# Rows of an attention output projection moved between the head loop and its tail, in a four-layer attention and Fourier kernel

## The chip, the cores and the metric

The kernel runs on one core of one Trainium2 chip. The metric is the device time of one execution in microseconds (us). A core has a matrix engine (TensorE, PE in the profile, with its weight loads shown apart as PEld), a vector engine (DVE), an activation engine (ACT), a GpSimd engine (POOL) and a sync engine (SP), from whose queue this kernel issues every transfer (DMA). The kernel writes out the order of the instructions on each engine by hand, and each engine works through its own list strictly in that order.

## The reference

Four layers over 2048 rows of 640 numbers: attention, Fourier mixing, attention, Fourier mixing, each on the normalised rows and added to them.

```python
def _A_ref(x, wqkv, wo):
    B, S, D = x.shape
    H = 32; Dh = D // H; W = 256
    ...
    scores = jnp.einsum("bhqd,bhkd->bhqk", q, k) * (Dh ** -0.5)
    ...
    mask = (idx[:, None] - idx[None, :] >= 0) & (idx[:, None] - idx[None, :] < W)
    scores = jnp.where(mask[None, None], scores, -1e9)
    p = _softmax(scores, axis=-1)
    o = jnp.einsum("bhqk,bhkd->bhqd", p, v)
    return (lambda x, *d: x.transpose(*d))(o, 0, 2, 1, 3).reshape(B, S, D) @ wo
...
x = x + _A_ref(_layernorm(x, axis=-1), A_wqkv, A_wo)
x = x + _B_ref(_layernorm(x, axis=-1), B_dft_seq_re, B_dft_seq_im, B_dft_hid_re, B_dft_hid_im)
x = x + _A_ref(_layernorm(x, axis=-1), A_wqkv, A_wo)
x = x + _B_ref(_layernorm(x, axis=-1), B_dft_seq_re, B_dft_seq_im, B_dft_hid_re, B_dft_hid_im)
```

## The kernel before

All products are made from numbers cut into a high and a low part, so a term `a @ b` takes three matmuls (high by high, high by low, low by high).

**The head loop** (`heads`). The 32 heads are taken in 8 groups of four (quads), and each quad in 16 blocks of 128 rows: 128 steps. In step t the loop makes, on PE, the transposed scores of block t (line 657), and the plain scores of the block 10 steps ahead (line 629), whose row maxima DVE takes (line 634). Every four steps the maxima of four blocks are transposed (line 642), copied by ACT to a small tile `mt`, and stored by a DMA (line 647) as an additional row of `qp`, the queries. The transposed scores need this row. ACT takes the exponentials (line 667), POOL zeroes what is outside of the window (lines 673 and 677), and PE multiplies by the values (line 692, 24 small matmuls, one group to a step) for the block one step back. In a trace the groups of line 692 count the steps.

**What fills PE in the steps.** Each step has one place, after the first half of its scores, where `fill(nf)` puts in other PE work: first the query and key projections of later heads (`project`, chunks 2 to 9 of 128 columns, matmuls on half the array, two at a time, line 255), then the output projection `@ wo`. The output projection has 16 row blocks and a contraction in five chunks (`CHUNKS`). Chunks 0 to 2 need heads 0 to 23 alone and are the "early" part (`partials`, `EARLY = 3`): one early row is a row block's 18 matmuls of 128x320 (36 on half the array), and DVE adds the result to the residual `y` (line 975), which a DMA has loaded (`load_y`, line 949). Chunks 3 and 4 need the last quads and are the "late" part (`late`, 12 matmuls to a row, lines 237 and 1069 or 1075); behind a late row follow the statistics and the normalisation for the Fourier layer. `fill(9)` (`LATE = 9`) puts in half an early row to a step. `BACK = 2` holds two early rows back until the loop has ended, and lets two late rows into it.

**Sets.** For four row blocks at a time `load_o` loads the heads' outputs (`x<-o_d` or `cr<-o_d`) and the reciprocals of their sums (`rr<-r_d`), multiplies them (POOL in the loop, DVE later, line 890) and cuts them. `prepare` loads and cuts the weights and the first set while the last projection chunk is made.

**Behind the loop** (`after_heads`). The early rows that are left, then late rows and the first units of the Fourier layer in turn (line 1380, 9 matmuls of 512 columns).

**Queues and order.** `post(n, f)` runs `f` n half steps later, `job` puts it in a lane that gives out one job for each engine and half step. All DMAs stand in one list on SP. Eight semaphores go round, so a DMA is not issued before the one eight places ahead of it in the list has landed. `pack` (line 592) loads the queries and keys of a quad from where the projection was stored (`qk_d<-c`, line 522), in four groups of three DMAs for each quarter of the rows; the list `due` says at which step each quarter is loaded and how much of the projection must be done by then.

## Time and profile before

| what | us |
|---|---|
| median of 3 runs (2198.74 to 2204.55) | 2202.13 |
| the profiled execution's own time | 2201.15 |
| its span, on which all the rows lie | 2199.4 |
| first attention layer: from the last projection work to the end of the head loop | 412 to 534 |
| first attention layer: late rows and first Fourier units | 534 to 600 |
| the same two stretches in the second attention layer | 1502 to 1624, 1624 to 1690 |
| PE busy in 412 to 440, of 28 us | 23.73 |
| PE busy in 650 to 700, of 50 us | 50.00 |

A row of a stretch gives, engine by engine, the busy time in it and the number of instructions; then the clock that TensorE was granted (1.00 is full), the share of the DMA engines' time and the GB/s. A row of the timeline gives the start, the time and the engine of an instruction or of several alike; in square brackets stands how long the engine had been idle before it, and what ended that.

### The profile page before, as it was taken

Reading aid. Unit: us, or ns where it says so; the run is one execution under the profiler, and the core shown is the slowest. Engines: PE = TensorE matmul, PEld = TensorE weight load, DVE = VectorE, ACT = ScalarE, POOL = GpSimd, SP = SyncE. Lnnn points to the kernel's source line nnn. Section 1 sums busy time; section 2 is a strip of 40 time slices with the busy share of each in tenths; the row PEclk is TensorE's granted clock in tenths of the full one; section 3 lists DMA queues with packets and bytes.
Section 4 is the critical chain, followed back from the end, with each engine's and each line's share of the span. In section 5 each row is a group of like instructions: output and inputs, shape, how many; then the busy total and the mean of one; then the engine's idle time right before and its main releaser. Section 6 shows DMA issues by size and latency. Waiting matters only on the chain.

```text
span 2199.4 us, 48840 instructions
## 1 busy us (share of the span) xinstructions
PE 2127.3 (97%) x17872; PEld 1785.7 (81%) x17872; DVE 1620.9 (74%) x3949; ACT 1139.1 (52%) x2125; POOL 969.0 (44%) x1568
## 2 busy tenths in 40 slices
PE   7999999998999999999999999999999999999999
PEld 7987777677868888889999777776777788888899
DVE  6358888786897868776661688887868968687776
ACT  3117776656554545552431377676655545455332
POOL 3037776765513223232330477677655133231324
PEclk9999999999999999999999999999999999999999
DMA  5556656785435453665646466668753354546643
GB/s 182 175 162 186 201 181 207 224 221 164 161 122 171 138 185 127 221 199 194 208 146 188 149 199 183 201 195 231 216 170 135 128 187 135 166 152 207 226 161 127
DMA packets 220175, 392.09 MB, mean 178 GB/s; under 512 B 39200, under 2 KB 85792, under 8 KB 219936
## 3 DMA queue, kind: packets, MB, share of 16 engines
q1 hardware_dynamic: 219936, 388.98, 56.4%
q8 instruction: 141, 2.31, 0.4%
q14 instruction: 98, 0.80, 0.1%
HBM read 273.94 MB, written 113.77 MB: 176 GB/s over the span
## 4 chain that ended last, share of the span: by engine, by line
PE 79%; DVE 7%; ACT 4%; DMA 4%; POOL 3%; issue 3%; SPq 0%; ACTq 0%; DVEq 0%; POOLq 0%
PE banks L1380 29%; PE banks L237 15%; PE banks L255 13%; PE banks L692 6%; PE banks L657 5%; PE banks L1668 5%; PE banks L629 4%; DVE banks L634 1%; DMA qp<-qk_d 1%; DVE qp L230 1%; ACT pt L667 1%; DMA qk_d<-c 1%; PE banks L339 1%; POOL rs L1084 1%; ACT big L1036 1%
## 5 line engine op out<-in xcount | busy, mean ns | idle before, releaser
L634 DVE CUSTOM_DVE_ANT_0 banks<-banks,mask 128x384 f32<-128x384 f32 (+2 forms) x1024 | 527.4, 557 | 120.2 <-PE banks L629 97.3
L667 ACT ACTIVATE pt<-banks 128x768 f32<-128x768 f32 (+2 forms) x512 | 393.7, 772 | 172.0 <-PE banks L657 66.4
L673 POOL TENSOR_SCALAR_AFFINE_SELECT pt<-pt 128x256 f32<-128x256 f32 x512 | 214.7, 420 | 217.5 <-ACT pt L667 197.8
L255 PE MATMUL banks<-big,wc 64*128 64x512 f32 x1920 | 270.8, 394 | 0.4 <-DVE pt L440 0.4
L657 PE MATMUL banks<-qp,kp 61*128 61x384 f32 (+2 forms) x1024 | 210.8, 382 | 24.8 <-DVE mc L634 17.6
L692 PE MATMUL banks<-pt,vq 128*32 128x128 f32 x5760 | 212.0, 278 | 3.5 <-ACT pt L667 3.5
L629 PE MATMUL banks<-kp,qp 60*128 60x384 f32 (+2 forms) x1024 | 205.6, 346 | 4.7 <-DVE mc L634 3.0
L255 PEld LDWEIGHTS banks<-big,wc 64*128 64x128 f32 x1920 | 185.7, 185 | 23.5 <-ACT x L542 1.5
L224 ACT ACTIVATE qp<-pt 128x512 fp32r<-128x512 f32 (+1 forms) x201 | 124.0, 625 | 140.2 <-DVE pt L1314 56.7
L677 POOL TENSOR_SCALAR_AFFINE_SELECT pt<-pt 128x256 f32<-128x256 f32 x448 | 194.0, 433 | 0.0
L692 PEld LDWEIGHTS banks<-pt,vq 128*32 128x32 f32 x5760 | 142.5, 110 | 51.4 <-issue 35.6
L230 DVE TENSOR_TENSOR qp<-pt,qp 128x512 fp32r<-128x512 f32 (+1 forms) x199 | 153.8, 781 | 41.0 <-ACT qp L224 39.3
L657 PEld LDWEIGHTS banks<-qp,kp 61*128 61x128 f32 x1024 | 108.6, 185 | 90.0 <-DVE mc L634 63.9
L1313 POOL TENSOR_TENSOR pt<-pt,pt 128x512 f32<-128x512 f32 x34 | 50.6, 1488 | 241.3 <-DMA pt<-c 166.4
L1380 PE MATMUL banks<-qp,big 128*128 128x512 f32 x648 | 154.5, 392 | 0.0
L224 ACT ACTIVATE c<-pt 128x512 fp32r<-128x512 f32 x144 | 89.3, 625 | 120.3 <-POOL pt L1300 56.4
L629 PEld LDWEIGHTS banks<-kp,qp 60*128 60x128 f32 x1024 | 123.8, 186 | 30.5 <-DVE mc L634 18.2
L634 DVE DVE_READ_ACCUMULATOR2_ANT mc<- 128x1 f32 x1024 | 145.0, 142 | 0.0
L1380 PEld LDWEIGHTS banks<-qp,big 128*128 128x128 f32 x648 | 121.5, 189 | 25.2 <-POOL qp L230 0.9
L230 DVE TENSOR_TENSOR c<-pt,c 128x512 fp32r<-128x512 f32 x142 | 113.9, 804 | 26.9 <-ACT c L224 24.3
L1380 PE MATMUL banks<-qp,xc 128*128 128x512 f32 x480 | 119.0, 394 | 6.5 <-DVE xc L230 3.7
L1380 PEld LDWEIGHTS banks<-qp,xc 128*128 128x128 f32 x480 | 90.2, 189 | 28.5 <-DVE xc L230 6.3
(248 smaller groups left out, 4464.5 us busy)
## 6 DMA issues: line engine op xcount, KB each, us to landing
pt<-c SPq DMA_DIRECT2D x188, 512.0 KB
qk_d<-c SPq DMA_DIRECT2D x80, 512.0 KB
kp<-qk_d SPq DMA_DIRECT2D x384, 80.0 KB
qp<-qk_d SPq DMA_DIRECT2D x384, 80.0 KB
kp<-u_d SPq DMA_DIRECT2D x32, 640.0 KB
o_d<-ou SPq DMA_DIRECT2D x64, 256.0 KB
x_d<-x SPq DMA_DIRECT2D x48, 320.0 KB
v_d<-pt SPq DMA_DIRECT2D x16, 768.0 KB
```

The lines of the kernel that those rows point to most:

```text
L224: nc.scalar.activation(hi, src, AF.Copy, scale=-1.0 if neg else 1.0)
L230: (eng or nc.vector).tensor_tensor(out=lo, in0=src, in1=hi.bitcast(F32), op=OP.subtract)
L237: self.nc.tensor.matmul(p, x, y, start=n == 0, stop=n == last)
L255: self.nc.tensor.matmul(ps[a], x[r], y[r], start=half + i == 0, stop=half == 1 and i == n - 1, skip_group_check=True)
L629: nc.tensor.matmul(p, qp[quad % 2][b:b + 60, z, qb * P:(qb + 1) * P], kp[quad % 2][b:b + 60, z, k0 * P:(qb + 1) * P], start=True, stop=True)
L634: nc.vector.tensor_tensor_reduce(out=p, in0=p, in1=self.mask[:, 384 - n * P:], scale=1.0, scalar=NEG, op0=OP.add, op1=OP.max, accum_out=mc ...
L657: nc.tensor.matmul(self.banks[:, banks[e], :n * P], kp[quad % 2][b:b + 61, z, kb * P:(kb + 1) * P], qp[quad % 2][b:b + 61, z, kb * P:(kb + ...
L667: nc.scalar.activation(pt[quad, kb][:, 2 * z:2 * z + 2, :n * P], self.banks[:, b0:b1 + 1, :n * P], AF.Exp, scale=SCALE)
L673: nc.gpsimd.affine_select(out=t[:, :, 0:P], in_=t[:, :, 0:P], pattern=[[0, 2], [1, P]], compare_op=OP.is_ge, fill=0.0, base=0, channel_mul ...
L677: nc.gpsimd.affine_select(out=t[:, :, 256:384], in_=t[:, :, 256:384], pattern=[[0, 2], [-1, P]], compare_op=OP.is_gt, fill=0.0, base=0, ch ...
L692: nc.tensor.matmul(self.banks[32 * h:32 * h + 32, bank, :P], vq[:, 96 * (kb % 4) + 21 * h:96 * (kb % 4) + 21 * h + 32], t[:, h, (qb - kb) ...
L1380: nc.tensor.matmul(self.banks[:, bk, :], p, b[q], start=start and m == 0, stop=stop and last and m == 2, skip_group_check=True)
```

## The change

The pieces of the diff in which the order of work is decided:

```diff
-LATE = 9
-BACK = 2
+LATE = (9, 5), (9, 9)
+BACK = 4
+FEW = 2
+LAST = [(c, sbs) for sbs in ((0, 1), (2, 3)) for c in (NCH - 2, NCH - 1)]
...
         for lane in self.lanes.values():
-            for _ in range(2 if self.lead else 1):
+            for _ in range(2 if self.lead or self.wide else 1):
...
     def project(self):
-        for c in range(2, NCH):
+        for c in range(2, NCH - 2):
...
-                if c == NCH - 1:
-                    self.prepare(sbs[0])
                 yield from self.pieces(c, sbs, "f" if lead else "m")
-        self.prepare(4)
+        for c, sbs in LAST:
+            if (c, sbs) == LAST[0]:
+                self.load_chunk(NCH - 1)
+                self.post(6, lambda: self.cut_chunk(NCH - 1))
+            if (c, sbs) == LAST[2]:
+                self.prepare()
+            yield from self.pieces(c, sbs, "m")
+        self.take_big(2, F32)
+        self.load_y(range(AHEAD_X))
...
-            if not self.left:
-                if self.part_t < NB - BACK:
-                    self.now = self.out if self.ready_part() else None
+            if not self.left and not self.open:
+                if self.late_t < 2 and self.ready_late():
+                    self.now = self.rest
                 else:
-                    self.now = self.rest if self.late_t < BACK and self.ready_late() else None
+                    self.now = self.out if self.part_t < NB - BACK and self.ready_part() else None
...
-                    size = -(-left // max(1, round(left / n)))
+                    size = -(-left // max(1, round(left / n[self.side])))
...
-                nf = LATE
+                nf = LATE[s >= steps]
...
         for i in range(n):
-            self.post(7, lambda i=i: self.job(lane, key, lambda: scale(i)))
+            self.post(7 if busy else 4, lambda i=i: self.job(lane, key, lambda: scale(i)))
...
+    def early_ks(self, sb):
+        return range(FEW if sb == 0 else EARLY)
+
+    def prepare(self):
+
+        self.take_big(0)
+        self.take_big(1)
...
+        def load(k):
+            raw = self.raw()
+            self.nc.sync.dma_start(raw, self.a["wo"][:, k, :])
+            self.post(6, lambda: self.cut_job("dve", "ew", *self.early_w[k], raw))
+
+        def first(k):
+            o["left"] -= 1
+            self.load_o(o, 0, k)
+        for at, f, k in ((3, load, 0), (5, first, 0), (7, load, 1), (9, first, 1), (11, load, 2)):
+            self.post(at, lambda f=f, k=k: f(k))
...
+    def late_ks(self, sb):
+        return range(len(self.early_ks(sb)), KC)
...
-        while self.one_part():
-            pass
         self.load_to(4 if self.late_t < 8 else 6)
+        while self.part_t < NB - 1:
+            self.one_part()
...
             if t == NB:
                 break
+            self.one_part()
```

The first four early rows take two chunks instead of three; the third chunk of these rows goes to their late part. The last four pieces of the projection are made in another order (both chunks of the first half of the rows, then both of the second), two quarters of `pack` come two steps later, and weights and first set are loaded sooner. A later early row is spread over three steps (18, 10 and 8 half-array matmuls) until the plain scores have ended. Four early rows are left behind the loop instead of two, and three of them stand right behind it. Two late rows go into the loop in place of early ones as soon as their set is marked ready, and in the last ten steps sets are multiplied three half steps sooner and lanes give out two jobs.

**SP's list around the residual rows.** In the list of transfers, `big` are the residual rows `y`, `kp` and `qp` the loads of `pack`, `vq` the values, `x` and `rr` the heads' outputs and their factors, `c` the pieces of the projection on their way to memory, `sm`, `o_d` and `r_d` the results of a finished quarter, `mt` the row maxima. Before, from `vq` to the next `mt`:

```order
L619 DMA vq_91<-v_d 128x384
L949 DMA big_5879<-x 128x640 x4
L592 DMA qp_105<-qk_d 20x2x512 x3
L522 DMA qk_d<-c 128x2x512
L709 DMA sm<-ou_98 128x1x16
L710 DMA o_d<-ou_98 128x512
L715 DMA r_d<-rc 128x16
L592 DMA kp_103<-qk_d 20x2x512 x3
L522 DMA qk_d<-c 128x2x512
L647 DMA qp_105<-mt 2x4x128 x2
```

Now, from the same `vq`, and after `sm`, `o_d` and `r_d` on to the same `mt`:

```order
L631 DMA vq_91<-v_d 128x384
L967 DMA big_5871<-x 128x640 x5
L875 DMA x<-o_d 128x1x512
L883 DMA rr_100<-r_d 128x1x512
L875 DMA x<-o_d 128x1x512
L604 DMA kp_560<-qk_d 20x2x512 x3
L528 DMA qk_d<-c 128x2x512
```

```order
L604 DMA qp_105<-qk_d 20x2x512 x3
L604 DMA kp_103<-qk_d 20x2x512 x3
L967 DMA big_5871<-x 128x640
L528 DMA qk_d<-c 128x2x512
L875 DMA x<-o_d 128x1x512
L883 DMA rr_101<-r_d 128x1x512
L659 DMA qp_105<-mt 2x4x128 x2
L604 DMA qp_105<-qk_d 20x2x512 x3
```

Between the `mt` ahead of this piece and the one that ends it stood 22 DMAs; now there are 32. Added are two residual rows, three `x`, two `rr` and one group of three from `pack`, and another group of `pack` stands behind the `mt` that stood ahead of it.

**PE in the first step without projection work.** Line 657 (now 669) are the transposed scores, 629 (641) the plain ones, 692 (704) the products with the values, `big,big` in line 255 (261) an early row. Before:

```order
L657 MATMUL banks<-qp_104,kp_103 128x384 x2
L629 MATMUL banks<-kp_560,qp_105 128x384 x2
L657 MATMUL banks<-qp_104,kp_103 128x384 x2
L629 MATMUL banks<-kp_560,qp_105 128x384 x2
L692 MATMUL banks<-pt_96,vq_92 32x128 x4
L692 MATMUL banks<-pt_97,vq_92 32x128 x4
L692 MATMUL banks<-pt_94,vq_93 32x128 x4
```

Now:

```order
L669 MATMUL banks<-qp_104,kp_103 128x384 x2
L641 MATMUL banks<-kp_560,qp_105 128x384 x2
L261 MATMUL banks<-big_5119,big_5120 128x320 x12
L669 MATMUL banks<-qp_104,kp_103 128x384 x2
L641 MATMUL banks<-kp_560,qp_105 128x384 x2
L704 MATMUL banks<-pt_96,vq_92 32x128 x4
L704 MATMUL banks<-pt_97,vq_92 32x128 x4
L704 MATMUL banks<-pt_94,vq_93 32x128 x4
```

Five such steps had no early work and the next 28 had 18 half-array matmuls each; now eight steps have 12, one has none, then come six rows of 18, 10 and 8, and four steps with 18.

**PE right behind the loop.** `big,big` and `big` are an early row, `qp,kp` a late one, line 1380 (now 1410) a Fourier unit. Before:

```order
L237 MATMUL banks<-big_5481,big_5482 128x320 x6
L237 MATMUL banks<-big_5481 128x320 x3
L237 MATMUL banks<-big_5481,big_5482 128x320 x6
L237 MATMUL banks<-big_5481 128x320 x3
L237 MATMUL banks<-big_5481,big_5482 128x320 x6
L237 MATMUL banks<-big_5481 128x320 x3
L237 MATMUL banks<-big_5481,big_5482 128x320 x6
L237 MATMUL banks<-big_5481 128x320 x3
L237 MATMUL banks<-qp_105,kp_560 128x320 x12
```

Now, from the third of the early rows on:

```order
L242 MATMUL banks<-big_5119,big_5120 128x320 x6
L242 MATMUL banks<-big_5119 128x320 x3
L242 MATMUL banks<-big_5119,big_5120 128x320 x6
L242 MATMUL banks<-big_5119 128x320 x3
L242 MATMUL banks<-big_5119,qp_105 128x320 x3
L242 MATMUL banks<-qp_105,kp_560 128x320 x6
L242 MATMUL banks<-big_5119,qp_105 128x320 x3
L242 MATMUL banks<-qp_105,kp_560 128x320 x6
L242 MATMUL banks<-big_5119,big_5120 128x320 x6
L242 MATMUL banks<-big_5119 128x320 x3
L242 MATMUL banks<-big_5119,big_5120 128x320 x6
L242 MATMUL banks<-big_5119 128x320 x3
```

Three early rows, a late row of 18 matmuls and the fourth early row stand ahead of the first Fourier unit, where two early rows and one late row of 12 stood. The units and the other late rows alternate as before.

More of the change, by code (lines that the diff above doesn't have):

```diff
@@ L841, in load_o @@
         o["left"] = o.get("left", 0) + 1
-        if not self.after and not all((q, sb) in self.stored for q in range(h0 // 4, h1 // 4)):
+        shared = k and CHUNKS[k - 1][:2] == (h0, h1)
+        free = next((i for i in range(3) if i not in self.rr_held), None)
+        if (shared and ("rr", sb, k - 1) not in self.turn or rr is None and not shared and free is None) or not self.after and not all(
+                (q, sb) in self.stored for q in range(h0 // 4, h1 // 4)):
             def again():
```

103 lines of the change are left out of this document (50 added, 53 removed).

## The prediction

> **What bounds the kernel now.** I read the page first, then the busy times by stretch, then PE's timeline and SP's queue where PE has gaps.
>
> ```profile
> PE 2127.3 (97%) x17872; PEld 1785.7 (81%) x17872; DVE 1620.9 (74%) x3949; ACT 1139.1 (52%) x2125; POOL 969.0 (44%) x1568
> ...
> 412.00:440.00 28.00, 23.73 (x318) 16.59 (x316) 20.93 (x75) 15.64 (x30) 17.02 (x38) 0.94 0.80 234
> 440.00:503.00 63.00, 58.03 (x914) 48.40 (x913) 52.70 (x176) 38.94 (x72) 42.58 (x91) 1.00 0.77 210
> 503.00:534.00 31.00, 27.90 (x434) 22.52 (x429) 14.08 (x30) 19.09 (x37) 19.70 (x41) 0.94 0.44 131
> 534.00:600.00 66.00, 61.48 (x331) 54.46 (x329) 56.42 (x139) 37.31 (x71) 35.55 (x43) 0.97 0.55 175
> 700.00:750.00 50.00, 50.00 (x222) 41.40 (x222) 37.30 (x59) 28.13 (x55) 8.30 (x6) 1.00 0.45 144
> 1502.00:1530.00 28.00, 23.72 (x315) 16.98 (x316) 20.80 (x73) 15.26 (x31) 16.79 (x38) 0.94 0.82 236
> ```
>
> PE sets the time; in the Fourier layer (700 to 750) it never rests. The gaps are where attention ends, 412 to 600, and there the change works. The second attention layer repeats the first (1502 to 1530 beside 412 to 440), so each term below counts twice.
>
> How long is a step, and how much of it is PE's own work? The groups of line 692 count steps:
>
> ```profile
> 165.93 0.42 PE L692 MATMUL banks<-pt,vq 128*32 128x128 f32 x8
> ...
> 378.36 0.86 PE L692 MATMUL banks<-pt,vq 128*32 128x128 f32 x24
> ...
> 412.35 0.86 PE L692 MATMUL banks<-pt,vq 128*32 128x128 f32 x24
> ...
> 425.52 0.86 PE L692 MATMUL banks<-pt,vq 128*32 128x128 f32 x24
> ...
> 439.20 0.86 PE L692 MATMUL banks<-pt,vq 128*32 128x128 f32 x24
> ...
> 440.45 1.49 PE L255 MATMUL banks<-big,big 64*128 64x320 f32 x18
> 441.77 0.34 PE L657 MATMUL banks<-qp,kp 61*128 61x384 f32 x2
> ...
> 442.23 0.86 PE L692 MATMUL banks<-pt,vq 128*32 128x128 f32 x24
> ...
> 502.85 0.86 PE L692 MATMUL banks<-pt,vq 128*32 128x128 f32 x24
> ```
>
> With projection work: 78 steps from 165.93 to 378.36, 2.72 us each. Without any: five steps from 412.35 to 425.52, 2.63 each. The step from 439.20 to 442.23 has no wait: 3.03, of which 18 half-array matmuls take 441.77 - 440.45 = 1.32, so the step's own work on PE is 1.71. The 18 steps from 442.23 to 502.85 take 60.62, 3.37 each. So an empty step wastes 0.9 us of PE though its busy time hardly shows it. The Trainium skill (Trainium Kernel Development and Optimization, Performance Expectations) calls matmul busy time a bad metric for this and weight-load busy a good one; the 97% and 81% of the page agree.
>
> The other gap is a wait for a transfer:
>
> ```profile
> 420.99 7.56 DMA qk_d<-c
> ...
> 428.61 3.23 DMA qp<-mt
> ```
>
> ```profile
> 413.33 1.17 SPq L647 DMA_DIRECT2D qp<-mt  x2
> ...
> 417.78 1.79 SPq L949 DMA_DIRECT2D big<-x  x4
> ...
> 422.18 0.61 SPq L709 DMA_DIRECT2D sm<-ou  x1
> ...
> 428.61 1.09 SPq L647 DMA_DIRECT2D qp<-mt  x2
> ```
>
> ```profile
> 431.97 0.45 PE L657 MATMUL banks<-qp,kp 61*128 61x384 f32 x2 [1.60 <-DMA qp<-mt]
> ...
> 434.00:435.00 1.00, 1.00 (x10) 1.00 (x9) 0.00 (x0) 0.00 (x0) 0.22 (x1) 0.50 0.64 170
> ```
>
> The `mt` at 428.61 is eight places behind the store of 420.99 and could not go before that had landed. PE has the row at 431.97. This is a gate: all later steps count from it. Behind it PE runs some 3.4 us at half clock (the 0.50), 1.7 us lost.
>
> **The change part by part**, for one attention layer.
>
> *The gate.* 32 transfers now stand between the two `mt` where 22 stood. Sizes and rate:
>
> ```profile
> DMA packets 2311, 3.88 MB, mean 259 GB/s; under 512 B 529, under 2 KB 673, under 8 KB 2306
> ...
> big<-x SPq DMA_DIRECT2D x6, 320.0 KB
> kp<-qk_d SPq DMA_DIRECT2D x15, 80.0 KB
> x<-o_d SPq DMA_DIRECT2D x4, 256.0 KB
> rr<-r_d SPq DMA_DIRECT2D x3, 256.0 KB
> ```
>
> Added: 2 x 320 + 3 x 256 + 2 x 256 + 3 x 80 = 2160 KB, 2.21 MB; at the 259 GB/s of 417 to 432, 8.5 us. Against that, the piece begins sooner, since an `x` and an `rr` that were issued in the 1.9 us ahead of 413.33 stand elsewhere now, and the old queue had some slack. Bounds 3.5 (half of the extra fits into slack) and 8.5; I take 6.0, nearer to the full price, because SP waited for landings from 422.18 on. PE reaches the gate with six steps of early work done, so it idles there, and these matmuls (27 full ones more than before) gain nothing by themselves: **+6.0**.
>
> *Three steps behind the gate.* Before, 442.23 - 431.97 = 10.3 with 18 matmuls each. Now 12, 12 and none: two steps of 2.80 (2.72, and 12 of 320 columns weigh 0.88 where 7.5 of 512 weighed 0.80), one of 2.63, and the same half clock of 1.7, 9.9: **-0.4**.
>
> *The 18 steps to 502.85.* Three steps to a row now carry 18 + 10 + 8 = 36, a mean of 12 a step, for which the steady rate gives 2.80: 50.4 for six rows instead of 60.6, **-10.2**. Bounds: PE's own work is 3 x 1.71 + 2.64 = 7.8 a row, 46.6; with the waits for DVE that the old steps had (next row, 4.7 us in 18 steps) kept in full, 9.0 a row, 54. So -14 to -6.6. Three rows less are made, 54 full matmuls of 0.147, 7.9 us, which go behind the loop.
>
> ```profile
> L657 PE MATMUL banks<-qp,kp 61*128 61x384 f32 x68 | 13.8, 391 | 4.8 <-DVE mc L634 4.7
> ```
>
> *The last ten steps.*
>
> ```profile
> 520.68 0.86 PE L692 MATMUL banks<-pt,vq 128*32 128x128 f32 x24
> ...
> 523.46 0.86 PE L692 MATMUL banks<-pt,vq 128*32 128x128 f32 x24 [1.07 <-ACT pt L667]
> ...
> 532.88 0.86 PE L692 MATMUL banks<-pt,vq 128*32 128x128 f32 x24
> ```
>
> Before: six full steps of 2.97 to 520.68, an empty one of 2.78, three to 532.88, 30.0 in all. Now four full, two empty, four with half a late row (nine full matmuls, 1.32, like an 18; I count 2.75): 11.9 + 5.6 + 11.0 = 28.4, **-1.6**. That the late set is multiplied sooner costs nothing while DVE has room, 14.08 of 31 us; otherwise the late rows wait and up to 2 us of this go.
>
> *Behind the loop.* Full matmuls in the loop: 28 x 9 + 24 = 276 before, 8 x 6 + 6 x 18 + 4 x 9 + 4 x 9 = 228 now. The 48 others come behind it:
>
> ```profile
> 535.09 1.04 PE L237 MATMUL banks<-big,big 128*128 128x320 f32 x6
> ...
> 536.41 1.04 PE L237 MATMUL banks<-big,big 128*128 128x320 f32 x6
> ...
> 541.79 1.14 PE L237 MATMUL banks<-qp,kp 128*128 128x320 f32 x6 [1.69 <-DVE big L975]
> ...
> 547.70 1.99 PE L237 MATMUL banks<-qp,kp 128*128 128x320 f32 x12 [0.95 <-ACT big L224]
> ...
> 569.14 2.67 PE L237 MATMUL banks<-qp,kp 128*128 128x320 f32 x12 [1.77 <-DVE x L1075]
> ```
>
> Nine matmuls take 1.32, one 0.147, 48 take 7.1. Against that stand 4.4 us of waits, and another half clock of 1.7 (the stretch has a clock of 0.97): 6.1 that work could fill. DVE, which PE waits for, has 56.42 of 66 us there; the second late set now goes through it before the loop ends, and the held rows give it 8 us at the start. I take 4.0 of it as filled (bounds 1.5 and 6.1): **+3.1**.
>
> Sum: 6.0 - 0.4 - 10.2 - 1.6 + 3.1 = -3.1 a layer, -6.2 for both. The profiled execution took 2201.15 (span 2199.4), so 2194.9 by it; the median of the runs is 0.98 above it: **2196**.
>
> *What I cost at nothing.* The loads of the weights and of the first set move from one block ahead of the early rows to several places some ten steps sooner; DVE's and POOL's work on them lies under PE's projections, and if it does not, a cut ahead of a row maximum lengthens a step or two there by what it takes itself. A quarter of `pack` now stands right behind the store that it reads, so SP stands still for the landing, 7.56 us at 420.99; behind it stand the results of a quarter and the first `mt` of the piece, which is needed five steps, some 13 us, later. If that slack is gone, the residual rows start later and the gate goes to its upper bound. In the Fourier units only buffers change places.
>
> A rule speaks against the change at the gate: the Trainium skill (TensorE: Matmul & The Clock Gate, Why this matters for your kernels) says that an idle gap of over some 3 us sends PE back to half clock. The 0.50 behind 431.97 agrees. By it, a longer wait and a second one ahead of it (for the residual rows, below) would cost one half-clock stretch more, 1.7 us a layer, and the sum would be -1.4 a layer, 2199.
>
> **The rivals.**
>
> *The queue does not bite.* If the extra transfers fit into SP's slack, the gate moves by 1 us only: -8.1 a layer, 2186. For it: DMA share is 0.80 in 412 to 440, not 1; against it: SP waits for landings from 422.18 on.
>
> *The queue becomes the bound.* The full 8.5, and ahead of it DVE's addition of the first early row, which now stands some two steps behind the last projection, while the first residual row landed only at 422.18 (that let `sm` go, eight places on); the row maxima of the next steps stand behind that addition. PE then rests twice, with a half clock of 1.7 for each, and the 18 steps fall by their lower bound: 8.5 + 3.4 - 0.4 - 6.6 - 1.6 + 3.1 = +6.4 a layer, 2215. With the other terms as I take them, the loss begins when the gate moves by more than 9.1 us. For it: the order, which is certain; against it: the rate, which the queue had not reached all the time.
>
> *The held rows do not do what they are held for.* Three of the four stand together right behind the loop, and the waits at 547.70 and 569.14 come later. If the waits all stay: 6.0 - 0.4 - 10.2 - 1.6 + 7.1 = +0.9 a layer, 2204.
>
> **How the numbers follow.** Chances: the sum 0.45 (own range 2189 to 2203: bounds that partly cancel), no bite 0.18, queue as bound 0.27, waits stay 0.10. A measurement of this kernel can tell about 0.3%, 6.6 us, from no change: faster means under 2195.5. Of the sum 0.21 is faster and 0.24 within; no bite is all faster; waits stay is 0.07 within and 0.03 slower; queue as bound is slower. Faster 0.39, same 0.31, slower 0.30. The range leaves out the outer parts of the two queue cases: 2185 to 2212.
>
> **What would show it.** The gate: line 669 of the seventh quad's third step starts at 438, not 432 (line 657 before), released by `mt` or the group behind it; at 433 or at 441 the first or the second rival holds. The steps: six rows in 50 to 51 us. Behind the loop: no wait over 1 us for line 995 or 1104 (the additions), and the stretch from the loop's end to the last late row some 3 us longer. I am wrong if PE waits in the Fourier layer instead (600 to 650 now), or if rows of the loop wait for a set that is marked ready but hasn't been cut.

## The result and the profile after

The changed kernel took 2230.82 us (median of 4 runs, 2227.03 to 2231.9), the kernel before 2201.95 us in the same comparison: a ratio of 1.0131, 95% interval 1.0118 to 1.0144. It is 29 us slower; the prediction said 2196, and 2212 at most. The profiled execution took 2231.64 (span 2229.9).

The busy times by stretch in the changed kernel, for the stretches shown of before (busy us and number of instructions of each engine, then granted clock, DMA share, GB/s):

```profile
412.00:440.00 28.00, 21.09 (x284) 16.83 (x280) 18.13 (x64) 13.24 (x26) 16.40 (x35) 0.84 0.80 234
440.00:503.00 63.00, 59.06 (x880) 46.17 (x879) 53.16 (x186) 40.72 (x74) 40.13 (x90) 0.96 0.73 206
503.00:534.00 31.00, 24.47 (x325) 18.56 (x317) 11.23 (x21) 18.39 (x34) 18.73 (x40) 0.83 0.53 152
534.00:600.00 66.00, 62.48 (x394) 56.86 (x393) 51.32 (x127) 32.19 (x62) 28.24 (x36) 0.97 0.51 165
700.00:750.00 50.00, 50.00 (x223) 41.42 (x222) 35.32 (x52) 23.64 (x47) 10.13 (x7) 1.00 0.56 182
```

The middle of the Fourier layer is as it was. In 412 to 440 and in 503 to 534 PE is busy for less of the time than before, 21.09 for 23.73 and 24.47 for 27.90, and the clock fell in both, from 0.94 to 0.84 and 0.83.

The first line of the page, beside the one of before (PE 2127.3) in the prediction:

```profile
PE 2141.7 (96%) x17752; PEld 1800.1 (81%) x17752; DVE 1619.3 (73%) x3947; ACT 1138.4 (51%) x2125; POOL 964.0 (43%) x1564
```

PE rests 16.1 us more than before (2229.9 - 2141.7 against 2199.4 - 2127.3), and it is busy for 14.4 us more, although it makes no more matmuls. The second part is clock: the mean granted clock of the execution fell from 0.994 to 0.985. So about half of the loss is waits, and about half is PE at work at half clock behind them.

To put the loss in its place, the groups of line 704 (692 before) are taken as a clock of steps. From the changed kernel's PE timeline, the ends of the stretches:

```profile
164.86 0.42 PE L704 MATMUL banks<-pt,vq 128*32 128x128 f32 x8
...
376.92 0.86 PE L704 MATMUL banks<-pt,vq 128*32 128x128 f32 x24
...
412.75 0.86 PE L704 MATMUL banks<-pt,vq 128*32 128x128 f32 x24
...
502.32 0.86 PE L704 MATMUL banks<-pt,vq 128*32 128x128 f32 x24
...
538.93 0.86 PE L704 MATMUL banks<-pt,vq 128*32 128x128 f32 x24
```

These are steps 0, 78, 90, 117 and 127 of the first attention layer; step 99 is at 449.76. Before, they were at 165.93, 378.36, 412.35, 502.85 and 532.88, step 99 at 442.23. The second attention layer has the same steps from 1270.54 on (1255.66 before), and the last stretch reaches to step 0 of the second attention layer or to the end. Each entry below is how much longer the stretch is than before, to about 0.1 us. Each kernel has one profile, and executions of one kernel lie up to some 10 us apart (before, in one comparison, 2196.64 to 2205.81), so 1 to 2 us in one stretch of one layer can be chance; what both layers show counts for more.

| stretch | forecast, us a layer | first layer | second layer |
|---|---|---|---|
| steps 0 to 78 | 0 | -0.4 | 0.0 |
| 78 to 90 (weights and first set loaded) | 0 | +1.8 | +3.1 |
| 90 to 99 (the gate and three steps) | +5.6 | +7.1 | +8.7 |
| 99 to 117 (the 18 steps) | -10.2 | -8.1 | -8.2 |
| 117 to 127 (the last ten) | -1.6 | +6.6 | +5.5 |
| behind the loop | +3.1 | +8.8 | +6.5 |
| sum | -3.1 | +15.8 | +15.6 |

Two stretches came out near the forecast. The last ten steps and the tail behind the loop did not, and they hold 6.6 + 1.6 + 8.8 - 3.1 = 13.9 of the 18.9 us that the first layer is off.

**The gate.** PE's timeline, DVE's, and SP's queue of the changed kernel, in this order:

```profile
421.17 0.58 PE L669 MATMUL banks<-qp,kp 61*128 61x256 f32 x2 [2.14 <-DVE mc L646]
...
439.28 0.69 PE L669 MATMUL banks<-qp,kp 61*128 61x384 f32 x2 [4.40 <-DMA qp<-mt]
```

```profile
419.76 0.82 DVE L995 TENSOR_TENSOR big<-banks,big 128x640 f32<-128x640 f32 x1 [1.60 <-DMA big<-x]
```

```profile
434.86 1.15 SPq L659 DMA_DIRECT2D qp<-mt  x2
```

The `mt` went at 434.86 instead of 428.61: 6.25 us later, where the forecast had 6.0. PE passes the gate at 439.28 instead of 431.97; the test on record gave 438 for the sum and 441 for the second rival. But PE waits twice. At 421 it waits for DVE's row maxima (line 646), which stand in DVE's list behind the first early row's addition, and that addition waits for its residual row: the second rival's mechanism. Around each wait PE's clock is at half for 6.8 us, 13.7 us together, where before it was for 3.4.

**The last ten steps.** PE's, ACT's and POOL's timelines of the changed kernel:

```profile
512.03 0.45 PE L669 MATMUL banks<-qp,kp 61*128 61x384 f32 x2 [1.86 <-ACT pt L679]
512.31 2.03 PE L261 MATMUL banks<-big,big 64*128 64x320 f32 x18
...
521.65 0.86 PE L704 MATMUL banks<-pt,vq 128*32 128x128 f32 x24 [1.88 <-ACT pt L679]
```

```profile
510.65 0.63 ACT L222 ACTIVATE big<-x 128x512 fp32r<-128x512 f32 x1 [1.85 <-POOL x L915]
511.18 0.79 ACT L679 ACTIVATE pt<-banks 128x768 f32<-128x768 f32 x1
...
520.27 0.63 ACT L222 ACTIVATE kp<-cr 128x512 fp32r<-128x512 f32 x1 [0.18 <-DVE cr L915]
520.80 0.79 ACT L679 ACTIVATE pt<-banks 128x768 f32<-128x768 f32 x1
521.50 0.62 ACT L222 ACTIVATE kp<-cr 128x512 fp32r<-128x512 f32 x1
522.02 0.80 ACT L679 ACTIVATE pt<-banks 128x768 f32<-128x768 f32 x1
```

```profile
509.90 0.72 POOL L915 TENSOR_TENSOR x<-x,rr 128x256 f32<-128x256 f32 x1
```

Here one reads two hops back. PE waits for an exponential (line 679). The exponential stands on ACT behind a cut of a set (line 222), and the cut waits for a multiplication of that set on POOL (line 915), which worked without a gap from 499 to 511. This is the last early set: the kernel multiplies it on POOL seven half steps after its load, as before, so only the place of the cut ahead of the exponential is new. Ten us later the first late set's cuts stand ahead of one exponential after the other, and the first two of them wait for DVE (0.18 us each). DVE, in which the prediction looked for room, is busy for only 11.23 of 31 us; it is ACT's order that the sooner work disturbs. The waits cost twice: of the ten steps 10.2 us are at half clock (mean 0.86), against 3.4 and 6.8 before (0.94 and 0.89 in the two layers).

**Behind the loop.** The double Fourier unit that ends the alternation with late rows (x18), before and in the changed kernel, and what follows it:

```profile
595.47 4.27 PE L1380 MATMUL banks<-qp,big 128*128 128x512 f32 x18
```

```profile
563.76 3.21 PE L242 MATMUL banks<-qp,kp 128*128 128x320 f32 x12 [2.05 <-DVE x L1104]
...
606.26 4.27 PE L1410 MATMUL banks<-qp,big 128*128 128x512 f32 x18
611.16 0.50 PE L1410 MATMUL banks<-c,big 128*128 128x512 f32 x1 [0.63 <-ACT c L229]
612.71 2.11 PE L1410 MATMUL banks<-c,big 128*128 128x512 f32 x8 [1.05 <-POOL c L235]
...
656.48 3.35 PE L1410 MATMUL banks<-qp,xc 128*128 128x512 f32 x7 [1.06 <-DVE xc L235]
```

From the loop's last group to this unit: 62.6 us before, 67.3 now, 4.7 more for 7.1 us of moved matmuls; in the second layer 59.8 and 67.4, 7.5 more. PE's waits there fell, from 4.4 and 3.4 us to 2.7 in both layers, but each layer now has a half clock, and before only the first had one. Behind this unit, in the Fourier units, which the forecast had at nothing, another 4.1 us were lost in the first layer, and 1.1 gained in the second. What appears there in the first layer stands in the kernel before in the second:

```profile
1688.63 0.50 PE L1380 MATMUL banks<-c,big 128*128 128x512 f32 x1 [0.66 <-ACT c L224]
1690.18 2.08 PE L1380 MATMUL banks<-c,big 128*128 128x512 f32 x8 [1.05 <-POOL c L230]
...
1733.92 3.15 PE L1380 MATMUL banks<-qp,xc 128*128 128x512 f32 x7 [0.99 <-DVE xc L230]
```

So it is not shown that the moved rows bring these waits.

### The profile page after: what moved, and what is told of

The parts are those of the page before. It is cut to its first block, busy times and chain, and to the rows that moved or that the text cites. A ratio compares the mean times of both kernels' runs of the same rounds, so it can differ in the third digit from the quotient of the medians.

```text
span 2229.9 us, 48548 instructions
## 1 busy us (share of the span) xinstructions
PE 2141.7 (96%) x17752; PEld 1800.1 (81%) x17752; DVE 1619.3 (73%) x3947; ACT 1138.4 (51%) x2125; POOL 964.0 (43%) x1564
## 4 chain that ended last, share of the span: by engine, by line
PE 78%; DVE 8%; DMA 5%; ACT 3%; POOL 3%; issue 3%; SPq 1%; ACTq 0%; DVEq 0%; POOLq 0%
PE banks L1410 28%; PE banks L242 17%; PE banks L261 11%; PE banks L704 7%; PE banks L669 5%; PE banks L641 5%; PE banks L1698 4%; DMA qp<-qk_d 1%; DVE banks L646 1%; DVE qp L235 1%; DMA kp<-qk_d 1%; DMA x<-wo 1%; PE banks L345 1%; POOL big L235 1%; ACT pt L679 1%
## 5 line engine op out<-in xcount | busy, mean ns | idle before, releaser
L641 PE MATMUL banks<-kp,qp 60*128 60x384 f32 (+2 forms) x1024 | 212.9, 351 | 7.0 <-ACT pt L679 3.9
L235 DVE TENSOR_TENSOR qp<-pt,qp 128x512 fp32r<-128x512 f32 (+1 forms) x201 | 161.9, 810 | 57.5 <-ACT qp L229 55.2
L1410 PE MATMUL banks<-qp,big 128*128 128x512 f32 x630 | 149.6, 392 | 0.0
```

The lines of the kernel that those rows point to most:

```text
L235: (eng or nc.vector).tensor_tensor(out=lo, in0=src, in1=hi.bitcast(F32), op=OP.subtract)
L641: nc.tensor.matmul(p, qp[quad % 2][b:b + 60, z, qb * P:(qb + 1) * P], kp[quad % 2][b:b + 60, z, k0 * P:(qb + 1) * P], start=True, stop=True)
L1410: nc.tensor.matmul(self.banks[:, bk, :], p, b[q], start=start and m == 0, stop=stop and last and m == 2, skip_group_check=True)
```

## The experiments

Every kernel was compared with the kernel before in runs on the same chip. The changed kernel has its ratio from its own comparison and is set beside the others by ratio. The stretches are those of the table above, first and second layer, from each kernel's profile; the last column counts the full matmuls that each has behind the loop beyond those of before.

| kernel | ratio to before (95%) | 78 to 90 | 90 to 99 | 99 to 117 | 117 to 127 | behind | moved |
|---|---|---|---|---|---|---|---|
| changed | 1.0131 (1.0118 to 1.0144) | 1.8, 3.1 | 7.1, 8.7 | -8.1, -8.2 | 6.6, 5.5 | 8.8, 6.5 | 48 |
| late_jobs | 1.0095 (1.0076 to 1.0113) | 0.9, 0.9 | 7.7, 5.7 | -8.0, -7.8 | -1.0, -3.0 | 12.5, 7.8 | 75 |
| one_job | 1.0084 (1.0058 to 1.0110) | 0.9, 0.9 | 6.3, 7.1 | -8.1, -7.7 | 2.3, 1.3 | 10.0, 8.4 | 57 |
| later_scale | 1.0110 (1.0092 to 1.0127) | 0.9, 1.5 | 9.2, 7.3 | -8.1, -8.1 | 1.9, 0.7 | 10.2, 10.5 | 66 |
| hold_rows | 1.0095 (1.0080 to 1.0110) | 0.9, 0.8 | -0.9, -0.2 | -2.6, -2.8 | 3.2, 1.1 | 11.3, 7.4 | 57 |
| two_y_ahead | 1.0130 (1.0113 to 1.0147) | 0.9, 0.9 | 4.2, 7.1 | -8.1, -8.2 | 6.6, 5.4 | 9.4, 8.7 | 48 |
| two_rows_back | 1.0092 (1.0077 to 1.0107) | 0.9, 1.0 | 7.4, 7.4 | -6.6, -8.2 | 3.7, 2.5 | 6.1, 3.1 | 30 |
| rows_in_two | 1.0140 (1.0122 to 1.0157) | 0.9, 3.5 | 8.3, 5.9 | -1.2, -1.9 | 1.3, -0.8 | 8.1, 6.2 | 48 |
| order_and_loads | 1.0075 (1.0058 to 1.0093) | 0.8, 0.8 | 1.7, 2.6 | 1.1, 0.2 | -1.5, -2.3 | 7.3, 5.1 | 0 |
| rows_first | 1.0064 (1.0043 to 1.0084) | 0.9, 0.8 | 0.5, 2.6 | 0.9, 0.1 | 1.2, -1.3 | 3.9, 3.0 | 0 |
| loads_only | 1.0015 (1.0003 to 1.0027) | 0.9, 1.0 | 2.0, 2.0 | 0.0, 0.0 | -1.5, -2.8 | 0.9, 0.4 | 0 |
| after_rows_first | 1.0118 (1.0093 to 1.0143) | 1.2, 0.8 | 6.7, 8.2 | -8.1, -8.2 | 4.2, 4.5 | 8.0, 8.1 | 48 |
| three_undone | 1.0052 (1.0034 to 1.0070) | 0.9, 0.8 | -0.1, -1.6 | -4.9, 0.0 | -5.7, -6.4 | 14.3, 14.9 | 84 |

**The last ten steps: late_jobs, one_job, later_scale.** The first undoes both parts of what the change does to late sets, the others one each.

```diff
-            for _ in range(2 if self.lead or self.wide else 1):
+            for _ in range(2 if self.lead else 1):
...
-            self.post(7 if busy else 4, lambda i=i: self.job(lane, key, lambda: scale(i)))
+            self.post(7, lambda i=i: self.job(lane, key, lambda: scale(i)))
```

In late_jobs and later_scale a set is also marked ready three half steps after its cut instead of one, as before.

> Only the third part is undone: in the last ten steps lanes give out one job per half step and late sets are multiplied seven half steps after their load. In the changed kernel the steps from 117 to 127 took 6.6 and 5.6 us more than before in the two layers. Theory A (the multiplications and cuts of the late sets stand ahead of the exponentials on ACT and DVE, PE waits up to 1.9 us for an exponential and then runs at half clock): these steps come back to what they took before, 30 us, and some 27 of the late matmuls (4 us) go behind the loop, where half of them fill waits: 2 to 4 us a layer, 2223 to 2227 us. Rival B (the last steps are long because of the early rows of 18 half-array matmuls that were pushed there by the late gate): no change, 2229 to 2233.

> Of the third part only the double lanes are undone (one job per half step); late sets are still multiplied sooner. Undoing both brought the steps 117 to 127 from +6.6 and +5.6 us to -0.9 and -3.0 against before, with 27 full late matmuls sent behind the loop. Theory A1 (two cuts in one half step stand ahead of an exponential): the last ten steps come to within 2 us of before's 30; 9 full matmuls (half a late row) go behind, 1.3 us: 4 to 6 us a layer better than the changed kernel, which measures 1.0131 of before: ratio 1.008 to 1.0095. Theory A2 (the sooner multiplication waits on DVE or POOL, whatever the lanes): the last ten steps stay 5 us longer, ratio 1.012 to 1.0135.

> Of the third part only the sooner multiplication is undone (seven half steps after the load again); lanes still give out two jobs. Theory A1 (two cuts ahead of an exponential): the last ten steps stay 4 to 6 us longer than before, ratio to before 1.011 to 1.0135. Theory A2 (the multiplication comes before its data have landed and holds the engine): they fall to within 2 us of before, 18 full matmuls go behind (2.6 us), ratio 1.0085 to 1.0105.

With both undone the steps 117 to 127 take 29.1 us instead of 36.6. Three of the four half late rows leave the loop (27 matmuls, 4.0 us), so 3.5 us were waits and half clock. The same ten steps of late_jobs on ACT:

```profile
520.57 0.62 ACT L222 ACTIVATE qp<-x 128x512 fp32r<-128x512 f32 x1
521.09 0.80 ACT L679 ACTIVATE pt<-banks 128x768 f32<-128x768 f32 x1
521.78 0.28 ACT L711 ACTIVATE ou<-banks 128x128 f32<-128x128 f32 x1
521.93 0.64 ACT L222 ACTIVATE kp<-cr 128x512 fp32r<-128x512 f32 x1
522.51 0.81 ACT L679 ACTIVATE pt<-banks 128x768 f32<-128x768 f32 x1
```

Each of these cuts stands between two exponentials and waits for nobody, and no wait of PE in these steps is over 1.4 us. Theory A holds and rival B falls: the 18s of steps 118 to 121 stand there unchanged. The gain by ratio, 0.36% or 4.0 us a layer, is the upper end of what was expected: the 27 matmuls cost 3.7 and 1.3 us more behind the loop. Between A1 and A2 there is no winner: with one part undone 4 to 5 us of these steps come back either way, with both 7.6 and 8.5; of these 1.3 (one_job), 2.6 (later_scale) and 4.0 us are matmuls that left the loop. The waits tell the two parts apart. PE's lists of later_scale and one_job:

```profile
513.47 0.44 PE L669 MATMUL banks<-qp,kp 61*128 61x384 f32 x2 [1.86 <-ACT pt L679]
```

```profile
517.67 0.86 PE L704 MATMUL banks<-pt,vq 128*32 128x128 f32 x24 [1.07 <-ACT pt L679]
```

The changed kernel's wait at 512.03 stands in later_scale, which keeps the double lanes, and is gone in one_job and late_jobs, in both layers: the double lanes make it. The one at 521.65 (1.88) takes both parts, for it is 1.07 in one_job and 0.74 in later_scale. later_scale stands near the changed kernel in time (1.0110, intervals that overlap) because 18 matmuls more went behind the loop at full price and its gate was 2 us longer in the first layer.

**The gate: hold_rows, two_y_ahead.**

```diff
-                    self.now = self.out if self.part_t < NB - BACK and self.ready_part() else None
+                    self.now = self.out if self.step >= 97 and self.part_t < NB - BACK and self.ready_part() else None
```

> The early rows start five steps later, where they started before (step 96), with their loads of residual rows and of the second set; all else as changed. In the changed kernel the steps 92 to 99 cost 7 and 8.5 us more than before. Theory A (the early rows that start five steps sooner bring their transfers ahead of the row maxima, and DVE's first addition waits for a residual row): the two waits of 2.1 and 4.4 us and their half clock go, 6 to 8 us a layer, less what is made later (up to 2 us): 2217 to 2224 us. Rival B (the waits come from the pack group and the set that stand elsewhere in SP's list whatever the rows do): the wait for the row maxima stays near 4 us, time 2227 to 2233.

```diff
-AHEAD_X = 4
+AHEAD_X = 2
```

> The early rows start where the change has them, but residual rows are loaded two rows ahead instead of four: 3 transfers of 320 KB fewer at the first piece. Theory A1 (bytes ahead of the row maxima): 0.98 MB less at some 260 GB/s, the wait for the maxima is 2 to 4 us shorter and DVE gets the first residual row about 1 us sooner: 3 to 5 us a layer, 2220 to 2225 us. Rival A2 (the places in the list, the ring of eight, not the bytes): under 1.5 us a layer, 2227 to 2231 us. If the rows now land too late for DVE, it gets slower than 2233.

Holding the rows takes the whole loss at the gate away: -0.9 and -0.2 against +7.1 and +8.7, with one wait for the maxima left:

```profile
431.50 0.69 PE L669 MATMUL banks<-qp,kp 61*128 61x384 f32 x2 [2.52 <-DMA qp<-mt]
```

Theory A of that run holds: the early rows bring it, not the `pack` groups that stand elsewhere. But the kernel gained only 0.36%, 8 us, half of what the gate gave. The 18 steps to 117 came out at -2.6 and -2.8 instead of -8.1 and -8.2, though they hold 48 full matmuls fewer than before, nearly the 54 of the changed kernel: a later `mt` is now waited for (1.6 us), and both layers have a half clock there (mean clock 0.97). Nine late matmuls more went behind the loop. Removing a stall at a gate lets what was waiting behind it become visible.

With two residual rows ahead instead of four the `mt` went at 431.93, 2.9 us sooner, and the first layer's gate fell to +4.2; the second's to +7.1. Two residual rows fewer stand ahead of this `mt`, so a row of 320 KB counts for some 1.5 us there (A1). But the ratio, 1.0130, shows no gain: a wait of 2.9 us for DVE's maxima stays, and behind the loop 0.6 and 2.2 us more were lost. The time is where rival A2 put it, though the `mt` moved as A1 said.

**Where rows are made: two_rows_back, rows_in_two.**

```diff
-BACK = 4
+BACK = 2
```

> Two early rows are held instead of four: one more row fits into the two empty steps 122 and 123, all else as changed. If PE in these steps has room as an empty step had before (0.9 us each), 18 full matmuls (2.6 us) behind the loop go and about 0.8 us come: 1 to 2 us a layer, 2227 to 2229 us. If ACT, not PE, sets these steps, the row is free and up to 2.6 us a layer go, 2225. If the held rows fill waits behind the loop as the prediction had it, the time is the same or up to 2 us a layer longer, 2230 to 2235.

```diff
-LATE = (9, 5), (9, 9)
+LATE = (9, 9), (9, 9)
```

> Only the spreading is undone: rows after the fourth take two steps of 18 half-array matmuls; the same twelve rows are made in the loop, eight in 96 to 115, then eight steps are empty. In the changed kernel the 18 steps to 117 took 2.92 each with a mean of 12, before 3.37 with 18; an empty one 2.63 to 2.8. If a step's time goes with its own filling, these twelve rows cost 16 x 3.37 + 8 x 2.7 = 75.5 us in steps 100 to 123, where spread they cost 18 x 2.92 + 4 x 3.0 + 2 x 2.7 = 70: 4 to 5 us a layer slower in these steps. Theory A (late jobs hold the last steps): in empty steps ACT has room, 2 to 3 us of this come back; ratio 1.013 to 1.0165. Rival B (the late 18s themselves make the last steps long): steps 117 to 127 fall to before's 30 us and the kernel is faster than the changed one, ratio under 1.011.

One row more in the loop (steps 122 and 123) gained 0.39%, 8.6 us, more than any of the three expectations. Behind the loop 2.7 and 3.4 us went, the price of 18 matmuls (2.6). And the last ten steps became shorter by 2.9 and 3.0 although they hold more work. The last ten steps of the changed kernel and of two_rows_back, first layer:

```profile
502.32:538.93 36.61, 29.24 (x386) 22.52 (x385) 16.25 (x31) 22.27 (x43) 21.96 (x44) 0.86 0.49 143
```

```profile
505.40:539.14 33.74, 27.86 (x421) 22.25 (x420) 17.13 (x33) 22.18 (x43) 22.05 (x44) 1.00 0.48 154
```

The clock is 1.00 instead of 0.86, in both layers, and half of the changed kernel's 10.2 us at half clock is some 5 us. With work in the two empty steps PE's wait of 1.88 us there is gone, and the half clock behind it. The wait of 1.85 us ahead of them stays (515.09), and that no half clock follows it is partly luck (last section). So the row in the two steps is not free on PE; the clock and the missing wait pay for it.

Without the spreading the steps 99 to 127 together are +0.1 and -2.7 against -1.5 and -2.6: 1.6 us in one layer, nothing in the other, and the intervals of the ratios overlap. Spreading is a nearly even exchange: undone, 36 full matmuls move from the last ten steps into the 18, which get longer by 6.9 and 6.3 us (8.1 - 1.2 and 8.2 - 1.9), and the last ten get shorter by 5.3 and 6.3. Rival B is half right: the last ten fell to 31.3 and 30.4 us, but the kernel did not get faster.

**Nothing but order: order_and_loads, rows_first, loads_only.** The first has all rows and late jobs as before:

```diff
+FEW = 3
+LATE = (9, 9), (9, 9)
+BACK = 2
...
+        for at, f, k in ((3, load, 0), (5, first, 0), (7, load, 1), (9, first, 1), (11, load, 2), (13, first, 2)):
```

together with the edits of late_jobs and hold_rows.

> All rows as before (three chunks, two steps each from step 96, two held back, one job, multiplication after seven half steps); what is left of the change is the order of the last projection pieces, two pack quarters two steps later, and weights and first set loaded sooner. With the rows held to step 96 the steps 90 to 99 were 0.3 to 0.8 us faster than before and the steps ahead of 90 0.7 to 1.0 us slower. Theory (the loss is in the rows and the late jobs alone): within 0.15% of before, 0.9985 to 1.0015. Rival (what stands sooner collides on SP and on ACT): over 1.003.

It was 0.75% slower than before though it moves no matmul of a row. The rival was right that order alone costs, but not in the place it named: 7.3 and 5.1 us are lost behind the loop. PE's and DVE's timelines there:

```profile
555.56 3.57 PE L242 MATMUL banks<-qp,kp 128*128 128x320 f32 x12 [4.65 <-DVE x L1104]
```

```profile
549.68 0.69 DVE L899 TENSOR_TENSOR pt<-pt,rr 128x512 f32<-128x512 f32 x1 [1.51 <-DMA rr<-r_d]
```

A late row's addition (line 1104) stands on DVE behind the multiplication of the third late set (line 899), which waits for its factors to land. Before, this multiplication stood behind six late rows, here it stands behind four, and it waited for nothing. Of PE's 4.65 us such waits are 1.9 (1.51 and 0.35); the rest is DVE's work on the set. Two lines of the change were suspected, and were undone in turn:

```diff
-        while self.part_t < NB - 1:
+        while self.part_t < NB:
             self.one_part()
```

> order_and_loads, with the two held rows both ahead of the first late row behind the loop, as before; the late set that is loadable sooner stays. PE's list is then the list of before. order_and_loads measured 1.0075 and lost 7.3 and 5.1 us behind the loop though no matmul was moved there. Theory C (a late row in between brings DVE's multiplication of the third late set ahead of its landing, 4.65 us of PE's waits, and the rows reach the Fourier units later): behind the loop within 1.5 us of before, ratio 1.0005 to 1.003. Rival D (the second late set, loaded sooner, does it): still 4 to 7 us a layer, ratio 1.005 to 1.008.

```diff
-                and (sb < 3 or self.late_t >= 6) and not (sb == 2 and self.late_o[-1]["left"])):
+                and (sb < 3 or self.late_t >= 6) and not (0 < sb < 3 and self.late_o[-1]["left"])):
```

> rows_first, and the second late set is loaded no sooner than before: PE's list and, behind the projection, all lists are those of before; what is left is where weights, first set and the last pack quarters are loaded, and the order of the last projection pieces. Theory C: as rows_first within 0.1%. Rival D: this one alone comes back to before. Either way the sooner loads show by themselves: order_and_loads had +0.8 us a layer ahead of step 90 and +2 at the gate, so ratio 1.0005 to 1.0025; under 1.0005 would mean that they cost nothing, as the prediction had it.

With the rows first, PE's list is the list of before, and by the profiles 3.4 and 2.1 us are back behind the loop (the ratios, 1.0075 and 1.0064, have intervals that overlap); the multiplication still waits, even longer, in DVE's list of rows_first:

```profile
554.09 0.69 DVE L899 TENSOR_TENSOR pt<-pt,rr 128x512 f32<-128x512 f32 x1 [3.64 <-DMA rr<-r_d]
```

With the second late set loaded no sooner the multiplication stands behind six rows again, the other 2.9 and 2.6 us go too, +0.9 and +0.4 are left, and the ratio falls from 1.0064 to 1.0015, with intervals apart. Rival D is shown; C has a part by the profiles alone. What remains, loads_only, is the price of the sooner loads alone: 1.0015 (1.0003 to 1.0027), 0.9 us a layer ahead of step 90, 2.0 at the gate, less 1.5 and 2.8 us in the last ten steps, where before's half clocks (0.94 and 0.89) are missing (1.00). Ahead of step 90 the cut of a weight chunk now stands on ACT ahead of an exponential. In loads_only it waits for nobody, and PE waits 0.23 us for the exponential. In the changed kernel, on ACT and PE:

```profile
387.57 0.74 ACT L222 ACTIVATE big<-x 128x640 fp32r<-128x640 f32 x1 [0.88 <-DMA x<-wo]
```

```profile
389.06 0.44 PE L641 MATMUL banks<-kp,qp 60*128 60x384 f32 x1 [1.15 <-ACT pt L679]
```

There the cut waits for its load, and the exponential behind it is late: the same pattern as in the last ten steps. This is what the changed kernel's profile has beyond 0.9 us. late_jobs has the same lists up to there and +0.9 in both layers, so it comes and goes between executions.

**Back to the changed kernel: after_rows_first, three_undone.** The first has the edits of rows_first and loads_only behind the loop of the changed kernel; the second has them together with those of late_jobs and hold_rows.

> The changed kernel with all four held rows ahead of the first late row behind the loop and the second late set loaded no sooner. The changed kernel loses 8.8 and 6.5 us behind the loop. Theory C (order): the 48 matmuls moved there then cost what the prediction had, 7.1 less some 4 of waits that they fill: 3 to 4 us a layer, the kernel gains 4 us a layer: ratio 1.008 to 1.0105. Rival E (moved matmuls cost their full price of 0.147 us wherever they stand, and the order is nothing beside it): 7 us a layer behind the loop, ratio 1.012 to 1.014. The set that is loaded later can also take a late row out of the loop (1 to 2 us a layer more).

> The changed kernel with its three losses undone at once: early rows held to step 96, one job per half step and the late sets multiplied after seven half steps, held rows first and the second late set no sooner behind the loop. What stays: two chunks for the first four rows, three steps for a later row, four rows held, the sooner loads. From the separate runs: ahead of step 90 +0.9, to 99 -0.5, to 117 -2.7, to 127 -1 to +1 us. If these losses are independent and the order behind the loop costs 4 to 6 us (C), some 75 matmuls more behind the loop cost 5 to 7 us: 2 to 5 us a layer slower than before, ratio 1.002 to 1.0045. If moved matmuls cost their full price there (E), 9 to 11 us: ratio 1.006 to 1.0085. Faster than before would mean that spreading the rows earns more than the 0.149 us a matmul that the steps to 117 show.

In the changed kernel the order behind the loop is worth nothing that can be told: 1.0118 beside 1.0131, overlapping intervals, and +8.0 and +8.1 behind the loop beside +8.8 and +6.5. The ratio's interval (1.0093 to 1.0143) holds both theories; the stretch behind the loop, 3 to 4 us by C and 7 by E, speaks for E. Four held rows are enough work to cover DVE's wait for the third set; PE waits 2.7 us for line 1104 from the loop's end to the double unit, 3.9 in after_rows_first, 7.1 in order_and_loads. So it looks as if of the two prices one is paid: the wait, or the matmuls that cover it. The last column of the table agrees: with 30, 48, 57, 66, 75 and 84 matmuls moved, the mean loss behind the loop is 4.6, 8.0, 9.3, 10.4, 10.2 and 14.6 us, 0.14 to 0.17 us each.

With all three undone the time is 1.0052 of before, between what C and E had. The losses in the loop are gone, 9.8 and 7.2 us are gained from step 78 to 127, and 14.3 and 14.9 us are lost behind it, where 84 matmuls x 0.147 = 12.3 were moved. None of the twelve kernels beats the kernel before.

## Why the prediction was wrong

*The last ten steps* are the step that failed most: "That the late set is multiplied sooner costs nothing while DVE has room." DVE had room. What is moved sooner is the multiplication and with it the cut, an ACT instruction, and behind that in ACT's list stand the exponentials for which PE waits. The double lanes, which make the first of the two long waits, have no term in the sum at all. I costed the job on the engine that is named in the diff and not on each engine that it touches. Forecast -1.6, measured +6.6 and +5.5; late_jobs brings -1.0 and -3.0, with 27 of the late matmuls sent behind the loop. The other half of the sentence, "otherwise the late rows wait", named the wrong thing that waits.

*Behind the loop*: "I take 4.0 of it as filled." Ahead of the double unit the waits fell by 1.7 and 0.8 us only, and no half clock went: each layer has one now. So the 7.1 us of matmuls cost 4.7 and 7.5 there, and with the Fourier units +8.8 and +6.5. The rival that all waits stay had the better number (+7.1) and a chance of 0.10; its mechanism is half right, for 2.7 us of waits are left. The waits are not fixed gaps that work can be poured into. The second set, loaded sooner, and the row in between made new ones (order_and_loads, with nothing moved, lost 7.3 and 5.1), and the moved matmuls mostly covered these. "In the Fourier units only buffers change places" was off by 4.1 us in the first layer, of which 1.6 are waits for `c` (0.63 + 1.05 + 0.42, where 0.53 stood before) and some 1.5 one half clock at 656; in the second layer 1.1 us were gained. Why the `c` operands are later was not settled: before has the first two of these waits and the half clock in its second layer, loads_only in its first. The sign of being wrong that names 600 to 650 thus came in one layer of two.

*The gate*: the size of the queue's delay was right, 6.25 measured for 6.0, which was a choice between 3.5 and 8.5 and so in part luck. Missed was that the second rival's first wait, DVE behind its residual row, comes with it: +7.1 and +8.7 for the gate and its steps where +5.6 was forecast. The forecast kept one half clock of 3.4 us at the gate; 13.7 us came, and the half clock behind 431.97 in before does not agree with a gap of over 3 us, as the prediction says: the waits ahead of it were 1.04 and 1.60 us. That rival's mechanism was right; its price for these steps, 8.5 + 3.4 - 0.4 = 11.5, was too high.

*The 18 steps* went as forecast within the bounds: -8.1 and -8.2 for -10.2. What was not seen is what the number means. 54 full matmuls fewer for 8.1 us is 0.150 each, and behind the loop one costs 0.147. The exchange is even by itself, and rows_in_two shows it for the spreading inside the loop. The prediction counted on the waste of an empty step, 0.9 us, as a gain to be had. But by its own figures the spread steps waste as much as the full ones did: 2.92 - 2.60 (a third of the 7.8 us of own work a row) is 0.32, and 3.37 - 3.03 is 0.34. That the exchange with the tail is even was not seen.

*Costed at nothing*: the sooner loads were 0.9 us a layer by themselves in nearly all kernels and 1.8 and 3.1 in the changed kernel's profile, of which 1.7 in the second layer is a half clock.

What held: the loss doubled over the layers (15.8 and 15.6), the middle of the Fourier layer stayed full, and the sign of each stretch but one, where the sum has a term. The test "no wait over 1 us on lines 995 and 1104" failed at 563.76 with 2.05, and "rows wait for a set" was looked for on PE instead of on ACT.

## What to carry to other kernels

Cost a moved job on every engine in its chain, and ask at each what stands behind it in that engine's list; an in-order engine that is half idle still delays everything behind one instruction that was put in before its operand is there. When work moves between places, compare its marginal price in both (here 0.150 and 0.147 us a matmul) before counting a wait as room. Count with a wait the half clock behind it, which here was about half of the loss. And try the new order with no work moved: here it lost 0.75% by itself, which no sum over moved work could show.

## What the runs showed of the hardware that was not expected

The half clock comes in pieces of one length. Windows of 1 us of the changed kernel around two of them (the column before the last two is the clock):

```profile
420.00:421.00 1.00, 0.00 (x0) 0.00 (x0) 1.00 (x4) 0.00 (x0) 0.70 (x2) 0.92 0.96 251
...
427.00:428.00 1.00, 1.00 (x14) 1.00 (x12) 0.87 (x3) 0.15 (x1) 0.41 (x1) 0.66 0.86 209
```

```profile
512.00:513.00 1.00, 0.97 (x12) 0.97 (x14) 0.00 (x1) 0.57 (x2) 0.77 (x2) 1.00 0.95 231
513.00:514.00 1.00, 1.00 (x12) 1.00 (x10) 0.00 (x0) 0.38 (x1) 0.55 (x2) 0.50 1.06 313
...
516.00:517.00 1.00, 1.00 (x14) 0.98 (x12) 0.00 (x0) 0.53 (x2) 0.46 (x2) 0.79 1.01 331
```

A mean of 0.92 over a microsecond is half clock in its last 0.16; so the first lasts from 420.84 to 427.68, 6.84 us, the second from 513.00 to 516.42, 3.42 us, half of that. The second starts 0.97 us after PE has work again, behind a gap of only 1.86 us (510.17 to 512.03); a gap of 1.32 at 505 had no such effect. The Trainium skill (TensorE: Matmul & The Clock Gate, What's actually happening) describes a free-running window of 3413 ns, and the 3.42 agrees. The gap of over some 3 us that the prediction cited from the same page is not needed here: 1.86 us in one window were enough. One such stretch costs up to 1.7 us, about 0.08% of the kernel, and whether a gap meets one depends on where the window lies. two_rows_back has nearly the same wait, idle from 513.24 to 515.09, and no half clock behind it. Its half clock at 562.15, counted back in 14 pieces of 3.413 us, puts a window's end at 514.36, inside that wait. So the same list can meet more pieces or fewer: the four executions of one_job took 2211.88 us at a mean clock of 0.993, and 2222.01 to 2223.83 at 0.988 and 0.989.
